# Attention scores and k^T v in four quadrants of the matmul array, with a new map of PSUM banks and a new issue order for the opening

## The chip, the core and the metric

The kernel runs on one core of one Trainium2 chip. The metric is device time in microseconds (us), launch to end. A core has five engines with queues of their own: TensorE (PE, matmuls), VectorE (DVE), ScalarE (ACT), GpSimd (POOL) and SyncE (SP, which issues the DMAs here). Matmuls write to PSUM, which DVE and ACT read.

## What is computed

A linear attention with a decaying state, then two MLPs, all in float32. Four batches, 8 heads, 768 steps, 48 channels a head; the attention's output is laid out as 3072 tokens of 384.

```python
for t in range(S):
    cur = einsum('bhd,bhe->bhde', u * k[t], v[t])
    y[t] = einsum('bhd,bhde->bhe', r[t], state + cur)
    state = w[t][..., None] * state + einsum('bhd,bhe->bhde', k[t], v[t])
x = y as (3072, 384)
h = x @ w_in;  x = (h * sigmoid(1.702 * h)) @ w_out          # d_ff 2048
h = x @ w2_in; solu = h * softmax(h)                         # d_ff 1024
out = (layernorm(solu) * g_ln) @ w2_out
```

## The kernel before, in words

The attention is done in chunks of 64 steps. A *unit* is two chunks of one batch, 128 tokens with all 8 heads; there are 24 units, six (UB) to a batch. Both chunks of a unit lie side by side on the partitions: the first chunk's channels on partitions 64 to 111, the second's on 0 to 47.

The steps of a unit, with the names by which the issue list calls them and the lines of their instructions: loads (Lrkw, Ln, La, Lb); the front, with the running product of the decays (F1, line 134, DVE), r scaled by it (F2 line 140 on POOL, F4 line 146 on DVE), its inverse (F3, lines 153 to 155) and k scaled by that (F5, line 162); the bonus of the diagonal (B on POOL, lines 177 and 178; BR on DVE; BV on POOL, line 201, into `vd`); the transpose of k (ST, `turn_k`, line 213) and its copy to SBUF (SK, `copy_k`, line 218, ACT); the scores k r (SA, `scores`, lines 226 and 227); the masked product that takes them out of PSUM (M0 and M1, `masked`, line 232, DVE); k^T v (D, `states`, lines 253 to 266, or in two parts DA and DB for the first four units); the update of the state (U1, U2, `update`, lines 283 and 286, DVE); the mix with v (X, `mix`, lines 296 and 297); its sum with the bonus (V, `total`, line 303, DVE); the transpose of the result (T, line 311); and its split in a high and a low half (O line 320 on ACT, OL line 326 on DVE). A star in the list, as in OL:2*, moves a DVE step to PE (lines 330 and 331 for OL) and ACT.

A float32 matmul of the program shows as two matmul rows and two weight loads in the profile, so 16 products of the scores are 32 rows.

The attention has three PSUM banks. `three` makes them of a double tile `two` and a single tile `one`: bank 0 is the upper half of `two`, bank 1 is `one`, bank 2 the lower half of `two`, and 3 stands for all of `two`. The dependencies between instructions are found by the framework from the tiles that they touch. From unit 6 on, k's transpose lies in bank 0, the scores in 1, the mix in 2, the result's transpose in 1, and k^T v in 2 and 0.

The first MLP (w_in, w_out) goes over blocks of units, `BLOCKS`: three of two units, then six of three. For each block and each of 16 slices f of d_ff: `rise` (h in the list, line 496, 9 matmuls), `gelu` (e, lines 504 and 506, ACT), `rest` (g, line 511, DVE) and `fall` (o, line 521, 9 matmuls). Its weights arrive as raw 64-bit words that are unpacked in the opening: Lw (load), N0 on ACT, N1 to N3 on DVE (lines 387 to 392), H on ACT, C on DVE (line 423).

Two things set the order. Up to the end of the third block each engine's queue follows `START`, a list written out by hand in the order of issue; it covers units 0 to 8 entirely, most of unit 9, and all unpacking. After that a loop over blocks 3 to 7 and f runs: at each f it issues rise, gelu, rest, then the attention steps that `steps_of` puts there, and then the fall of two slices before. For unit i, `one` (transpose of k, copy, scores of unit i+1; mix of unit i; masked products of i+1; sum of i) stands at f = 1, 6 or 11, and `two` (transpose of the result of i; k^T v of i+1; split of i; update of i+1) three slices later. So the scores of units 10 to 23 are issued in the loop, those of 6 to 9 by the list. The second MLP follows with the whole core to itself, and the change doesn't touch it.

Of the kernel before, what the change touches and what calls it, by code (L numbers as in the profile page):

```python
# [11 lines left out]
ALU = mybir.AluOpType  # L12
# [3 lines left out]
H, D, C = 8, 48, 64  # L16
HD = H * D
# [26 lines left out]
C:4 N0:7 H:5 N2:6 F3:4 h0:4 V:3* La:4 T:3 O:3 o0:1 OL:3* N3:6 o0:3 h1:0 F5:4 F4:4 SA:4 ST:4 N1:7 e0:4 e1:0 g0:4 Lw:8  # L44
h1:1 C:5 g1:0 Lw:9 N2:7 o1:0 h1:2 H:6 N0:8 N1:8 N3:7 SK:4 o0:4 e1:1 H:7 N2:8 g1:1 C:7 Lw:10 La:5 Ln:4 o1:1 N3:8 N0:9
e1:2 N1:9 g1:2 h1:3 e1:3 N2:9 N0:10 D:4 Lb:5 g1:3 h1:4 N3:9 N1:10 e1:4 H:9 o1:3 Lrkw:5 Lrkw:6 C:6 h0:5 e0:5 Lw:12 g1:4
o1:4 h1:5 o1:2 M0:4 e1:5 Lw:11 g0:5 h1:6 U1:4 N2:10 B:4 BR:4 o0:5 BV:4 N3:10 Lw:13 g1:5 h1:7 e1:6 e1:7 H:10 M1:4 X:4
H:8 g1:6 o1:6 F1:6 N0:12 h0:6 e0:6 g1:7 o1:7 h0:7 U2:4 o1:5 C:9 C:10 g0:6 o0:6 C:8 N1:12 N0:11 F1:5 e0:7 g0:7 h1:8
h0:8 La:6 V:4 T:4 F3:5 Ln:5 e1:8 e0:8 g1:8 g0:8 o0:7 O:4 h0:9 N2:12 N0:13 OL:4 e0:9 g0:9 N1:11 N1:13 N2:11 o1:8 N3:12
h1:9 h0:10 e1:9 g1:9 o0:8 o0:9 e0:10 Lw:15 H:12 N3:11 H:11 h1:10 o1:9 e1:10 F4:6 F2:6 F2:5 F4:5 g0:10 F5:5 o0:10 N0:15  # L50
ST:5 C:11 h0:11 g1:10 C:12 N2:13 B:5 h0:12 SK:5 e0:12 e0:11 D:5 F3:6 N3:13 SA:5 g0:11 g0:12 Lw:14 N0:14 o1:10 N1:14
# [17 lines left out]
class Attention:  # L69
# [150 lines left out]
    def scores(self, i):  # L220
        nc, s = self.nc, self.st[i]
# [629 lines left out]
```

## Time and profile before

| | us |
|---|---|
| median of 3 runs | 766.41 |
| lowest and highest | 765.92, 767.46 |
| the profiled execution | 765.8 |
| its span in the profile | 763.7 |
| PE busy, of the span | 745.3 |
| DVE busy | 497.4 |
| ACT busy | 305.0 |
| POOL busy | 154.8 |

The opening (the list) goes from 0 to about 178 us, the loop with the attention and the first MLP to about 495, the last block of the first MLP to about 527, the second MLP to the end. In the profile PE is the matmuls and PEld the weight loads beside them. A row of the order in time gives the start, the length, engine, line, operation, output and inputs, the number of instructions merged, and in brackets the idle time of the engine before it and what ended it.

### The profile page before, as it was taken

How to read it: one execution, taken by the hardware profiler on the slowest of the kernel's cores; microseconds unless marked ns; L12 is line 12 of the kernel's file. 1: busy time of each engine (PE TensorE's matmuls, PEld its weight loads, DVE VectorE, ACT ScalarE, POOL GpSimd, SP SyncE). 2: the span in 40 equal slices, each digit the busy share in tenths (PEclk: the TensorE clock that was granted, in tenths of full speed). 3: DMA queues.
4: the chain of work that ended last, by engine and by line, in shares of the span. 5: the costliest groups of instructions: out<-in, count | busy, mean ns of one | idle time of the engine just before them, and what ended most of it. 6: DMA issues, size and time to landing. Idle time of an engine off the chain costs nothing.

```text
span 763.7 us, 15400 instructions
## 1 busy us (share of the span) xinstructions
PE 745.3 (98%) x6350; PEld 700.5 (92%) x6350; DVE 497.4 (65%) x849; ACT 305.0 (40%) x660; POOL 154.8 (20%) x158
## 2 busy tenths in 40 slices
PE   4899999999999999999999999999999999999998
PEld 3679999999999999999999999999999999999987
DVE  8989998885656665556466562388655555555553
ACT  2455453333222322322322322466544444444443
POOL 5530403622222222222022220031000000000000
PEclk9999999999999999999999999999999999999999
DMA  8656733324221222222222100342000000000000
GB/s 276 195 204 187 219 126 94 95 74 121 74 73 48 62 67 72 73 73 66 55 75 73 38 6 2 112 137 83 1 22 21 22 21 22 22 21 22 21 32 32
DMA packets 26102, 58.03 MB, mean 76 GB/s; under 512 B 3408, under 2 KB 18768, under 8 KB 26032
## 3 DMA queue, kind: packets, MB, share of 16 engines
q1 hardware_dynamic: 26032, 57.04, 25.2%
q8 instruction: 50, 0.82, 0.4%
q14 instruction: 20, 0.16, 0.1%
HBM read 52.31 MB, written 4.72 MB: 75 GB/s over the span
## 4 chain that ended last, share of the span: by engine, by line
PE 95%; DVE 3%; DMA 1%; issue 1%; ACT 0%; SPq 0%; DVEq 0%
PE acc L521 27%; PE h L496 26%; PE o L614 13%; PE left L561 7%; PE right L561 6%; PE att L296 3%; PE att L226 3%; PE right L601 1%; PE left L601 1%; PE att L213 1%; PE att L253 1%; PE att L311 1%; PE att L262 1%; DVE P L134 1%; DMA x2b<-in_w 1%
## 5 line engine op out<-in xcount | busy, mean ns | idle before, releaser
L521 PE MATMUL acc<-gh,w 128*128 128x384 f32 (+1 forms) x864 | 223.2, 322 | 0.0
L496 PE MATMUL h<-xTh,w 128*128 128x384 f32 (+1 forms) x864 | 180.1, 318 | 0.0
L504 ACT ACTIVATE gh<-h 128x384 fp32r<-128x384 f32 (+1 forms) x144 | 65.6, 456 | 271.3 <-PE h L496 263.9
L511 DVE TENSOR_TENSOR gl<-h,gh 128x384 fp32r<-128x384 f32 (+1 forms) x144 | 73.1, 510 | 145.5 <-ACT h L506 145.0
L521 PEld LDWEIGHTS acc<-gh,w 128*128 128x128 f32 x864 | 152.6, 189 | 2.3
L496 PEld LDWEIGHTS h<-xTh,w 128*128 128x128 f32 x864 | 142.8, 189 | 1.1 <-ACT w L421 0.5
L521 PE MATMUL acc<-gl,w 128*128 128x384 f32 (+1 forms) x432 | 137.2, 317 | 0.3 <-DVE gl L511 0.3
L496 PE MATMUL h<-xTl,w 128*128 128x384 f32 (+1 forms) x432 | 90.4, 317 | 0.0
L521 PEld LDWEIGHTS acc<-gl,w 128*128 128x128 f32 x432 | 81.6, 189 | 0.5 <-DVE gl L511 0.5
L496 PEld LDWEIGHTS h<-xTl,w 128*128 128x128 f32 x432 | 72.0, 189 | 0.0
L140 POOL TENSOR_TENSOR R<-rkw,P 64x512 f32<-64x512 f32 x24 | 30.7, 1281 | 202.2 <-DVE P L134 163.4
L614 PE MATMUL o<-w,xTh 128*128 128x384 f32 x384 | 70.5, 334 | 0.0
L614 PEld LDWEIGHTS o<-w,xTh 128*128 128x128 f32 x384 | 67.0, 188 | 0.2
L506 ACT ACTIVATE h<-h 128x384 f32<-128x384 f32 (+1 forms) x144 | 65.0, 451 | 0.0
L201 POOL TENSOR_TENSOR vd<-vs,dg 64x384 f32<-64x384 f32 x48 | 43.4, 904 | 98.4 <-PE att L311 61.4
L591 POOL TENSOR_TENSOR sm<-sm,mhalf 128x1 f32<-128x1 f32 x24 | 13.2, 548 | 218.6 <-DVE sm L590 218.6
L614 PE MATMUL o<-w,xTl 128*128 128x384 f32 x192 | 43.0, 346 | 0.0
L586 ACT ACTIVATE e<-q,sm 128x1024 f32<-128x1024 f32 x24 | 27.7, 1153 | 29.9 <-DVE sm L589 29.4
L561 PE MATMUL right<-w,x2h 128*128 128x512 f32 x144 | 37.1, 392 | 0.0
L561 PE MATMUL left<-w,x2h 128*128 128x512 f32 x144 | 37.0, 392 | 0.0
L226 PE MATMUL att<-R,rkw 48*64 48x64 f32 x368 | 27.1, 225 | 8.8 <-DVE rkw L162 8.8
L226 PEld LDWEIGHTS att<-R,rkw 48*64 48x64 f32 x368 | 23.9, 138 | 11.7 <-DVE rkw L162 8.8
(158 smaller groups left out, 1252.0 us busy)
## 6 DMA issues: line engine op xcount, KB each, us to landing
rkw<-in_rkw SPq DMA_DIRECT2D x22, 676.4 KB, 5.4
x2b<-in_w SPq DMA_DIRECT2D x16, 768.0 KB, 4.9
vs<-in_vn SPq DMA_DIRECT2D x48, 96.0 KB, 4.4
nr<-in_nat SPq DMA_DIRECT2D x24, 192.0 KB, 3.3
nk<-in_nat SPq DMA_DIRECT2D x24, 192.0 KB, 2.4
out<-ob SPq DMA_DIRECT2D x24, 192.0 KB, 1.9
raw<-in_w2o SPq DMA_DIRECT2D x8, 384.0 KB, 3.5
v<-in_v2n SPq DMA_DIRECT2D x24, 96.0 KB, 2.0
```

The costliest lines, as they stand in the source:

```text
L140: (e or self.nc.gpsimd).tensor_tensor(out=heads(R1[0:64]), in0=heads(s["rkw"][0:64, 0:HC]), in1=heads(s["P"])[0:64, :, 0:C], op=ALU.mult)
L201: nc.gpsimd.tensor_tensor(out=heads(vd[q:q + 64]), in0=heads(vt[q:q + 64]), in1=dg[q:q + 64].unsqueeze(2).to_broadcast([64, H, D]), op=ALU ...
L226: nc.tensor.matmul(out=A[0:64, c], lhsT=kt[64:112, c], rhs=R0[64:112, c], start=True, stop=True)
L296: mm(out=y[0:64, e], lhsT=s["R0"][0:112, c], rhs=s["vs0"][0:112, e], start=one, stop=one or h == 7)
L496: nc.tensor.matmul(out=h_ps, lhsT=W1[f][:, ws + c * 128:ws + (c + 1) * 128], rhs=xs[:, c, tok], start=n == 0, stop=n == 8)
L504: nc.scalar.activation(out=gh, in_=h_ps, func=AF.Gelu_apprx_sigmoid)
L506: return nc.scalar.activation(out=h_ps, in_=h_ps, func=AF.Gelu_apprx_sigmoid)
L511: nc.vector.tensor_tensor(out=gl_, in0=g, in1=gh.bitcast(F32), op=ALU.subtract)
L521: nc.tensor.matmul(out=a, lhsT=W1[f][:, ws + e * 128:ws + (e + 1) * 128], rhs=gs, start=first and n == 0, stop=last and n == 2)
L561: nc.tensor.matmul(out=h_ps[:, b * 512:(b + 1) * 512], lhsT=xs[:, c], rhs=W2I[c][wb][:, b * 512:(b + 1) * 512], start=n == 0 and c == 0, s ...
L586: nc.scalar.activation(out=e, in_=q, func=AF.Square, bias=sm[:, 3:4], accum_out=sm[:, 4:5])
L614: nc.tensor.matmul(out=O[i], lhsT=(lo if n == 2 else hi)[:, f * 128:(f + 1) * 128], rhs=W2O[f][n == 1], start=n == 0 and f == 0, stop=n == ...
```

## The change

`QUADS = UB` marks unit 6. From there on, the scores of heads 0 to 3 are written to the first 256 columns of bank 2 and those of heads 4 to 7 to the first 256 of bank 0, and the four products of one turn (two chunks, two groups of heads) use four different quadrants of the array: rows 64 to 111 or 0 to 47, columns 0 to 63 or 64 to 127. The masked product of a chunk is done in two instructions of four heads. The mix goes to columns 256 to 447 of the same two banks, and k's transpose to bank 1. For k^T v without parts (units 4 to 23) the four products of a pair of heads are issued in turn, where before two loops of two followed each other. `START` is ordered anew, with the same entries.

```diff
     def turn_k(self, i):
-        s["kT"] = self.bank(i, 0)
+        s["kT"] = self.bank(i, 0 if i < QUADS else 1)
...
     def scores(self, i):
-        A = s["A"] = self.bank(i, 1)
-        for h in range(H):
-            c = slice(h * C, (h + 1) * C)
-            nc.tensor.matmul(out=A[0:64, c], lhsT=kt[64:112, c], rhs=R0[64:112, c], start=True, stop=True)
-            nc.tensor.matmul(out=A[64:128, c], lhsT=kt[0:48, c], rhs=R1[0:48, c], start=True, stop=True)
...
+        P, Q = self.bank(i, 2)[:, 0:4 * C], self.bank(i, 0)[:, 0:4 * C]
+        s["A"] = [[(P[0:64], 0, 4), (Q[64:128], 4, 4)], [(P[64:128], 0, 4), (Q[0:64], 4, 4)]]
+        for h in range(4):
+            c, d = slice(h * C, (h + 1) * C), slice((h + 4) * C, (h + 5) * C)
+            mm(out=P[0:64, c], lhsT=kt[64:112, c], rhs=R0[64:112, c], start=True, stop=True)
+            mm(out=P[64:128, c], lhsT=kt[0:48, c], rhs=R1[0:48, c], start=True, stop=True)
+            mm(out=Q[0:64, c], lhsT=kt[0:48, d], rhs=R1[0:48, d], start=True, stop=True)
+            mm(out=Q[64:128, c], lhsT=kt[64:112, d], rhs=R0[64:112, d], start=True, stop=True)
...
     def masked(self, i, b):
+        for a, h, n in s["A"][b]:
+            a = a.rearrange("p (h t) -> p h t", h=n)
+            m = self.mask[q:q + 64] if h == 0 else self.mask[64 - q:128 - q]
+            self.nc.vector.tensor_tensor(out=heads(R[q:q + 64])[:, h:h + n], in0=a,
+                                         in1=m.unsqueeze(1).to_broadcast([64, n, C]), op=ALU.mult)
...
     def states(self, i, chunk=None):
+        if first:
+            for p in range(4):
+                mm(out=Dx[64:112, c], lhsT=kTs[0:64, p, 64:112], rhs=vs0[0:64, e], start=True, stop=True)
+                mm(out=Dx[0:48, c], lhsT=kTs[64:128, p, 0:48], rhs=vs1[64:128, o], start=True, stop=True)
+                mm(out=Dy[0:48, c], lhsT=kTs[0:64, p, 0:48], rhs=v2[0:64, p], start=True, stop=True)
+                mm(out=Dy[64:112, c], lhsT=kTs[64:128, p, 64:112], rhs=v2[64:128, p], start=True, stop=True)
+            return
...
     def mix(self, i, e=None):
-        y = s["y"] = self.bank(i, 1 if i < UB else 2)
+            s["y"] = y = self.bank(i, 3).rearrange("p (b c) -> p b c", b=2)[:, :, 4 * C:4 * C + 4 * D]
+            y = [y[:, h // 4, (h % 4) * D:(h % 4 + 1) * D] for h in range(H)]
...
 START = """
-U2:5 Lrkw:0 Lrkw:1 La:0 F1:0 F2:0 F3:0 F4:0 F5:0 F1:1 F4:1 F3:1 Ln:0 Lcst SA:0 M0:0 ST:0 F5:1 F2:1 SA:1 SK:0 Lw:1 N0:1
-Lb:0 N1:1 B:0 BR:0 BV:0 Lw:0 Ln:1 N2:1 N0:0 N1:0 La:1 DA:0 U1:0* ST:1 DB:0 SK:1 N2:0 Lrkw:2 M1:0 B:1 Ln:2 B:2 N3:0
-X:0* Lb:1 U2:0* V:0* T:0 O:0 F1:2 H:0 M0:1 F4:2 Lw:2 DA:1 U1:1* OL:0* N0:2 DB:1 Lrkw:3 BR:1 BR:2 C:0* M1:1 F3:2 Lb:2
-BV:1 X:1* V:1* Lw:3 U2:1* T:1 N1:2 O:1 F5:2 ST:2 N2:2 La:3 La:2 N3:1 Lw:4 SK:2 OL:1* N3:2 Lw:5 F2:2 SA:2 F1:3 H:2 H:1
-F3:3 h0:0 e0:0 g0:0 DA:2 U1:2* N0:3 C:1* h0:1 DB:2 M0:2 BV:2 Ln:3 M1:2 X:2* Lrkw:4 N1:3 N2:3 e0:1 F4:3 F2:3 N0:4 N3:3
-Lw:6 N0:5 Lb:3 g0:1 F5:3 H:3 C:2* h0:2 U2:2* N1:4 ST:3 B:3 V:2* T:2 O:2 N1:5 N2:4 o0:0 C:3 e0:2 h0:3 e0:3 N3:4 N2:5
-SK:3 OL:2* F1:4 F2:4 g0:2 g0:3 SA:3 BR:3 DA:3 o0:2 N0:6 U1:3* DB:3 Lw:7 M1:3 M0:3 N1:6 N3:5 U2:3* BV:3 X:3* Lb:4 H:4
...
+Lrkw:0 F1:0 F3:0 F2:0 F4:0 F5:0 SA:0 Lrkw:1 F1:1 F3:1 Ln:0 Lcst ST:0 B:0 Lw:1 N0:1 M1:0 F5:1 M0:0 La:0 Ln:1 F4:1 F2:1
+N1:1 SK:0 Lb:0 DA:0 Lw:0 BR:0 La:1 U1:0* DB:0 B:1 Ln:2 SA:1 ST:1 BR:1 N2:1 U2:0* N0:0 N1:0 N2:0 N3:0 M1:1 BV:0 SK:1
+X:0* V:0* T:0 Lb:1 DA:1 O:0 H:0 OL:0* C:0* N3:1 Lrkw:2 U1:1* DB:1 F1:2 M0:1 B:2 BR:2 U2:1* Lw:2 N0:2 BV:1 X:1* Lrkw:3
+V:1* F3:2 N1:2 T:1 O:1 OL:1* F5:2 N2:2 F4:2 ST:2 N3:2 Lw:3 F1:3 N0:3 N1:3 La:2 SK:2 h0:0 e0:0 g0:0 Lb:2 Ln:3 N2:3 Lw:4
+DA:2 U1:2* F2:2 F4:3 F2:3 H:2 H:1 SA:2 M0:2 M1:2 C:1* Lw:5 h0:1 F3:3 DB:2 U2:2* Lrkw:4 BV:2 X:2* B:3 e0:1 Lb:3 N0:4
+V:2* g0:1 N3:3 Lw:6 C:2* N1:4 h0:2 T:2 F5:3 N2:4 H:3 C:3 La:3 N0:5 N1:5 o0:0 O:2 h0:3 e0:2 N3:4 Lw:7 ST:3 N2:5 F1:4
+g0:2 BR:3 OL:2* SA:3 M1:3 SK:3 e0:3 DA:3 U1:3* o0:2 M0:3 DB:3 F2:4 g0:3 H:4 C:4 N0:6 La:4 N0:7 U2:3* N1:6 N3:5 N2:6
...
```

`total` and `turn` follow the new places; units 0 to 5 keep theirs.

## Rows read from the trace of the kernel before

**Rows 1.** The page's part 1: busy us, share of the span, instructions.
```profile
PE 745.3 (98%) x6350; PEld 700.5 (92%) x6350; DVE 497.4 (65%) x849; ACT 305.0 (40%) x660; POOL 154.8 (20%) x158
```
**Rows 2.** The page's part 4: shares of the chain that ended last, by line.
```profile
PE acc L521 27%; PE h L496 26%; PE o L614 13%; PE left L561 7%; PE right L561 6%; PE att L296 3%; PE att L226 3%; PE right L601 1%; PE left L601 1%; PE att L213 1%; PE att L253 1%; PE att L311 1%; PE att L262 1%; DVE P L134 1%; DMA x2b<-in_w 1%
```
**Rows 3.** Busy time by stretch: stretch and us, then busy us of each engine.
```profile
0.00:60.00 60.00, 45.42 (x548) 34.51 (x549) 53.28 (x73) 26.08 (x50) 28.59 (x26) 1.00 0.69 218
60.00:178.00 118.00, 117.69 (x1383) 114.82 (x1382) 104.30 (x164) 50.92 (x127) 35.33 (x32) 1.00 0.44 132
178.00:495.00 317.00, 316.90 (x2969) 306.07 (x2969) 176.12 (x279) 95.29 (x230) 68.41 (x68) 1.00 0.23 63
```
**Rows 4.** Waits of PE, 0 to 190 us: waiter, awaited: us, times, longest.
```profile
PE att L226 <- DVE rkw L162: 8.8, 1, 8.8
...
PE att L330 <- ACT kTs L218: 1.2, 1, 1.2
```
**Rows 5.** Order in time, PE: scores of unit 16, of unit 11, and their mixes.
```profile
306.80 0.27 PE L226 MATMUL att<-R,rkw 48*64 48x64 f32 x1
...
306.90 0.22 PE L226 MATMUL att<-R,rkw 48*64 48x64 f32 x1
...
307.73 0.22 PE L227 MATMUL att<-R,rkw 48*64 48x64 f32 x1
307.97 0.26 PE L296 MATMUL att<-vs,R 112*64 112x48 f32 x1
...
202.90 0.22 PE L227 MATMUL att<-R,rkw 48*64 48x64 f32 x1
203.04 0.26 PE L296 MATMUL att<-vs,R 112*64 112x48 f32 x1
```
**Rows 6.** Order in time, PE: k^T v of one unit.
```profile
296.12 0.24 PE L253 MATMUL att<-vs,kTs 64*48 64x48 f32 x1
...
296.20 0.20 PE L253 MATMUL att<-vs,kTs 64*48 64x48 f32 x1
...
296.35 0.24 PE L262 MATMUL att<-v,kTs 64*48 64x48 f32 x1
...
296.43 0.20 PE L253 MATMUL att<-vs,kTs 64*48 64x48 f32 x1
296.43 0.20 PE L262 MATMUL att<-v,kTs 64*48 64x48 f32 x1
296.44 0.20 PE L255 MATMUL att<-vs,kTs 64*48 64x48 f32 x1
296.44 0.20 PE L264 MATMUL att<-v,kTs 64*48 64x48 f32 x1
296.47 0.20 PE L253 MATMUL att<-vs,kTs 64*48 64x48 f32 x1
...
296.71 0.20 PE L264 MATMUL att<-v,kTs 64*48 64x48 f32 x1
```
**Rows 7.** Order in time, ACT: the copies of k's transpose beside Rows 5.
```profile
307.38 0.54 ACT L218 ACTIVATE kTs<-att 128x448 f32<-128x448 f32 x1
...
202.41 0.54 ACT L218 ACTIVATE kTs<-att 128x448 f32<-128x448 f32 x1
```
**Rows 8.** Order in time, DVE: after the scores of unit 16.
```profile
307.99 1.39 DVE L232 TENSOR_TENSOR R<-att,cc 64x512 f32<-64x512 f32 x2
309.42 0.56 DVE L303 TENSOR_TENSOR vd<-att,vd 128x384 f32<-128x384 f32 x1
313.46 0.56 DVE L511 TENSOR_TENSOR gl<-h,gh 128x384 fp32r<-128x384 f32 x1 [3.48 <-ACT h L506]
```
**Rows 9.** Groups by line and shape, DVE: count, busy us, mean ns.
```profile
L511 DVE TENSOR_TENSOR gl<-h,gh 128x256 fp32r<-128x256 f32 x48 | 19.7, 417 | 7.7 <-ACT h L506 7.2
...
L390 DVE SCALAR_TENSOR_TENSOR x2a<-x2b,x2a 128x768 uint32<-128x768 uint32 x16 | 15.9, 994 | 0.1
```
**Rows 10.** Order in time, POOL: a bonus product in the opening.
```profile
11.60 1.93 POOL L177 TENSOR_TENSOR nr<-nr,nk 128x384 f32<-128x384 f32 x1
```

More of the change, by code (lines that the diff above doesn't have):

```diff
@@ L23 @@
 VDB = 1
+QUADS = UB
 DFF2 = NF2 * 128
@@ L47 @@
[L47 to L51, printed above, removed]
@@ L220, in scores, with masked @@
     def scores(self, i):
-        nc, s = self.nc, self.st[i]
+        mm, s = self.nc.tensor.matmul, self.st[i]
         kt, R0, R1 = s["kt"], s["R0"], s["R1"]
-        A = s["A"] = self.bank(i, 1)
-        for h in range(H):
-            c = slice(h * C, (h + 1) * C)
-            nc.tensor.matmul(out=A[0:64, c], lhsT=kt[64:112, c], rhs=R0[64:112, c], start=True, stop=True)
-            nc.tensor.matmul(out=A[64:128, c], lhsT=kt[0:48, c], rhs=R1[0:48, c], start=True, stop=True)
-    def masked(self, i, b, e=None):
+        if i < QUADS:
+            A = self.bank(i, 1)
+            s["A"] = [[(A[0:64], 0, H)], [(A[64:128], 0, H)]]
+            for h in range(H):
+                c = slice(h * C, (h + 1) * C)
+                mm(out=A[0:64, c], lhsT=kt[64:112, c], rhs=R0[64:112, c], start=True, stop=True)
+                mm(out=A[64:128, c], lhsT=kt[0:48, c], rhs=R1[0:48, c], start=True, stop=True)
+            return
[7 more added lines that the diff above has]
+            mm(out=Q[64:128, c], lhsT=kt[64:112, d], rhs=R0[64:112, d], start=True, stop=True)
+    def masked(self, i, b):
         s, q = self.st[i], 64 * b
         R = s["R1" if b else "R0"]
-        (e or self.nc.vector).tensor_tensor(out=heads(R[q:q + 64]), in0=heads(s["A"][q:q + 64]),
-                                            in1=self.mask[q:q + 64].unsqueeze(1).to_broadcast([64, H, C]), op=ALU.mult)
+        for a, h, n in s["A"][b]:
[3 more added lines that the diff above has]
+                                         in1=m.unsqueeze(1).to_broadcast([64, n, C]), op=ALU.mult)
     def states(self, i, chunk=None):
@@ L261, in states @@
             o, c = slice((2 * p + 1) * D, (2 * p + 2) * D), slice(p * D, (p + 1) * D)
-            mm(out=Dy[0:48, c], lhsT=kTs[0:64, p, 0:48], rhs=v2[0:64, p], start=first, stop=first or p == 3)
-            if chunk is None:
-                mm(out=Dy[64:112, c], lhsT=kTs[64:128, p, 64:112], rhs=v2[64:128, p], start=True, stop=True)
-            else:
-                mm(out=Dx[0:48, c], lhsT=kTs[64:128, p, 0:48], rhs=vs1[64:128, o], start=False, stop=p == 3)
+            mm(out=Dy[0:48, c], lhsT=kTs[0:64, p, 0:48], rhs=v2[0:64, p], start=False, stop=p == 3)
+            mm(out=Dx[0:48, c], lhsT=kTs[64:128, p, 0:48], rhs=vs1[64:128, o], start=False, stop=p == 3)
     def update(self, i, b, e=None):
@@ L289, in mix @@
         mm, s = self.nc.tensor.matmul, self.st[i]
-        y = s["y"] = self.bank(i, 1 if i < UB else 2)
         one = e is None
+        if i < QUADS:
+            s["y"] = y = self.bank(i, 1)[:, 0:HD]
+            y = [y[:, h * D:(h + 1) * D] for h in range(H)]
+        else:
+            s["y"] = y = self.bank(i, 3).rearrange("p (b c) -> p b c", b=2)[:, :, 4 * C:4 * C + 4 * D]
+            y = [y[:, h // 4, (h % 4) * D:(h % 4 + 1) * D] for h in range(H)]
         if e is not None:
-            mm(out=y[:, 0:HD], lhsT=self.ident, rhs=s["vd"], start=True, stop=False)
+            mm(out=s["y"], lhsT=self.ident, rhs=s["vd"], start=True, stop=False)
         for h in range(H):
             c, e = slice(h * C, (h + 1) * C), slice(h * D, (h + 1) * D)
-            mm(out=y[0:64, e], lhsT=s["R0"][0:112, c], rhs=s["vs0"][0:112, e], start=one, stop=one or h == 7)
-            mm(out=y[64:128, e], lhsT=s["R1"][:, c], rhs=s["vs1"][:, e], start=one, stop=one or h == 7)
+            mm(out=y[h][0:64], lhsT=s["R0"][0:112, c], rhs=s["vs0"][0:112, e], start=one, stop=one or h == 7)
+            mm(out=y[h][64:128], lhsT=s["R1"][:, c], rhs=s["vs1"][:, e], start=one, stop=one or h == 7)
     def total(self, i, e=None):
-        s = self.st[i]
-        y, vd = s["y"][:, 0:HD], s["vd"]
+        y, vd = self.st[i]["y"], self.st[i]["vd"]
+        if i >= QUADS:
+            vd = vd.rearrange("p (b c) -> p b c", b=2)
         if e is None:
@@ L308, in turn @@
         s = self.st[i]
-        s["xT"] = self.bank(i, 2 if i < UB else 1)
+        s["xT"] = self.bank(i, 2 if i < QUADS else 1)
         for c in range(3):
```

38 lines of the change are left out of this document (21 added, 17 removed).

## Prediction, made before the changed kernel was run

> **What bounds the kernel now.** I read the page's busy table first, then the chain of work that ended last, then busy time by stretch, and only then the order in time of single steps. The page shows TensorE (PE) busy 745.3 of 763.7 us and VectorE (DVE) 497.4 [rows 1]; in the chain, lines 521 and 496 (the first MLP) hold 53% and the attention's products hold the shares that this change touches: line 226 (scores) 3%, line 253 and 262 (k^T v) 2% [rows 2]. Busy time by stretch says where a saved PE microsecond counts: from 178 to 495 us PE is busy 316.90 of 317.00 us while DVE has 176.12, so there the PE alone sets the pace; from 60 to 178 us it is busy 117.69 of 118.00; in the first 60 us only 45.42 [rows 3]. The waits of PE put 8.8 of those 14.6 idle us before the first product, which needs the loads and scans of unit 0, and 1.2 us in one wait on line 330 [rows 4]. So the kernel is PE-bound from about 60 us on, and behind that an opening that waits.
>
> "Busy" hides one thing: a small matmul's row is 0.20 to 0.27 us long, but the next begins much sooner. Costs below are therefore taken from start to start.
>
> **Scores, units 6 to 23.** Before, 16 logical products (32 matmul rows, two for each) alternate between lines 226 and 227, that is between two quadrants of the array. They start from 306.80 to 307.73, 0.93 us: a first interval of 0.10, then (307.73 - 306.90) / 14 = 0.059 us for each pair [rows 5]. Each quadrant thus takes a new matmul every 59 ns. In the change each of four quadrants gets 8 rows in place of 16. If a quadrant keeps its 59 ns with three neighbours active, first to last start is 0.10 + 6 x 0.059, and about 0.02 for the stagger, 0.47 us. Gain 0.46 us a unit, times 18 units 8.3 us.
>
> Whether four quadrants run at once is seen in the kernel before, in k^T v. Its first loop (lines 253, 255) and its second (262, 264) use different quadrants, and the second starts at 296.35 while the first still has rows to go. Between 296.43 and 296.47 all four lines are active, and line 253 still starts every 0.04 us (296.43, 296.47) as it did alone [rows 6]. Four starts fall into 10 ns there. So neighbours cost nothing that this view shows, and products into the same columns of the array and different banks (253 with 264, 255 with 262) go together, as the new scores need.
>
> **k^T v, units 4 to 23.** Because the loops overlap only near the end, the 32 rows start from 296.12 to 296.71, 0.59 us [rows 6]. Taken in turn from the start, each quadrant has 8 rows: 0.08 + 6 x 0.045 + 0.02 = 0.37 us. Gain 0.22 us, times 20 units 4.4 us. In the opening one of these units already overlaps with its neighbour's scores, so I take 4.3.
>
> **Where the banks go.** Before, k's transpose goes to one half of the double tile, and the mix to the other half. The first matmul of the mix starts at 307.97, 0.24 us after the last score, against 0.15 us at 202.90 to 203.04 [rows 5]; the copy of k's transpose (line 218, ScalarE) starts at 307.38 and takes 0.54 us, so it ends at 307.92, 0.05 us before the mix; the one at 202.41 ends at 202.95 [rows 7]. So the mix waits for that copy in five of the 14 units of the loop (0.24 there, 0.15 in the other nine), and would wait in all of them if the scores alone became shorter: this wait is next in line. The change moves the transpose to the single tile, which the mix no longer touches. I take the wait as gone: 5 x 0.09 = 0.45 us, and 0.15 us stays between scores and mix. If it stays, the scores gain almost nothing (a rival below).
>
> **The new wait, on DVE.** Scores and mix now lie in the same two banks, and the masked products of unit i+1 (DVE) stand behind the mix of unit i. They used to start at 307.99, as the mix began [rows 8]; now they start when it ends. The mix would begin at 307.97 - 0.55 = 307.42 (0.46 and 0.09, above) and takes, at the same 0.059 us a pair and 0.22 us for the last row, 1.15 us, so they start near 308.6. They also become four of 64x256 in place of two of 64x512 (1.39 us for the two [rows 8]). The nearest row to a 64x256 from PSUM is line 511 with 128x256, 417 ns [rows 9]: 4 x 0.42 = 1.67 us, 0.28 more a unit; bounds are 1.39 (nothing more) and 2.8 (each as long as now). Behind them queue the sum of line 303 and then the next low half of the GELU (line 511). DVE was idle 3.48 us before that one, at 313.46 [rows 8]. The shift is 0.6 + 0.3 = 0.9 us and that GELU comes 0.55 earlier, together 1.5 us, so it is covered; at 2.8 us it is 2.6, and 0.9 is left. Cost 0 on the path; without that idle time it would be 0.9 us a unit. The scores now write where the previous unit's k^T v lay, which its two updates read; those end two steps of the loop earlier, and the transpose waited for the same reads before. No transfer moves in the loop.
> The page "PSUM — Partial Sum Buffer" of the Trainium skill, section "PSUM bank collisions raise a hardware error", asks for a guard by bank and quadrant, not by address. By that rule the masked products may not start during the mix, although their columns are disjoint; that costs the 1.1 us of the mix on DVE and nothing on PE.
>
> **The opening, nine units set anew.** The new list has the same 564 entries, and the same 45 changes between attention and MLP on PE. I compared queue by queue what stands ahead of the same step. By row durations DVE has about 28.3 us of work before the first rise (h0:0) against 29.2, and 32.3 against 30.2 before the second; by the fourth both have 39.4. PE loses the scores of unit 2 before the first rise, but gets them before the second. One stall goes by construction: OL:2, behind SK:3 in the old list, waited 1.2 us for it (line 330 on 218 [rows 4]); in the new list it stands ahead. On POOL the bonus of unit 1 now stands ahead of unit 0's bonus times v, which seeds the first mix; a bonus is two products, the first of which took 1.93 us in the opening [rows 10], so up to 3.9 us. SP gets unit 0's v behind a weight block, Lw:1, but its first reader comes only after a transpose and a copy. So bounds: at best the 14.6 - 8.8 = 5.8 us of idle time are won back, at worst the 3.9 us of that bonus come onto the path. I take -1.0: the stall removed, less some 0.2 of slips, since the other shifts nearly cancel.
>
> **Sum.** -8.3 - 4.3 - 0.45 - 1.0 = -14.0 us on the profiled execution's 765.8, so 751.8. Its time lies 0.6 below the median of the three runs, 766.41, so the median should go to 752.4 us. A change of 0.2% (1.5 us) is about what a measurement of this kernel can tell from none.
>
> **Rivals.**
> *Matmuls are paced, not quadrants.* If PE can't start them faster than k^T v shows on average, 0.59 / 31 = 19 ns, scores need 31 x 0.019 = 0.59 us: gain 0.34 x 18 = 6.1, k^T v none, the rest as above, -7.6: 758.8. The four starts in 10 ns speak against it; that the burst lasts only three or four rounds speaks for it. 9%.
> The page "TensorE: Matmul & The Clock Gate" of the Trainium skill, section "Wait — 56ns, not 53.3ns?", states such a floor: start to start never below about 25 ns. By that the scores would need 0.78 us and the whole change would give 762.3 (an estimate from that page); the trace disagrees already with 19 ns on average.
> *The mix still waits for the copy of k's transpose.* Then the scores' gain turns into that wait: only 4.3 + 1.0, 761.1. The old bank map speaks for such a link, the new one against it, since the tiles differ. 6%.
> *The opening pays.* POOL's bonus puts 3.9 us on the path in place of -1.0: 757.3. 7%.
> *Slower than before.* The place is the opening, the mechanism DVE: it is busy 53.28 of 60 us there [rows 3], so each weight block whose unpacking on DVE (three steps, 0.99 us for one [rows 9]) is put ahead of an awaited step costs about 3.0 us. Eating the 13 us of the other terms takes more than four such slips; five (15 us) end at 768.4. The counts ahead of the same rises differ by 2.1 at most, against that. 4%.
> The forecast itself has 74%, with its own range 749 to 756: 18 units at 0.42 to 0.50, and an opening between -4 and +2.
>
> **How the numbers follow.** The forecast's range and the paced case and the paying opening lie between 748.5 and 759.0; outside are the mix that still waits (6%), the slower case (4%) and the tails of the forecast, some 8% together. Faster by over 0.2% 0.94, since all cases but the last lie below 764.9; within 0.2% 0.02; slower 0.04.
>
> **What would show it.** Lines of the new scores: 32 rows within 0.47 us; 0.93 or 0.59 says wrong or paced. Rows of k^T v: 0.37 us, all four lines from the start. The first row of the mix 0.15 us after the last score in every unit, and no wait on line 218. The masked products starting after the mix, at about 0.42 us each, and still no PE wait after 60 us. The first 384-wide rise, at 177.9 us before, some 4 us earlier (1.8 scores, 1.2 k^T v, 1.0 opening). The forecast is wrong if quadrants slow each other (intervals over 59 ns) or if the PE stands idle in the opening for longer than 14.6 us.

## The result, and the profile after

The changed kernel takes 753.26 us (median of 5 runs, 752.37 to 754.38) against 766.09 (765.76 to 767.46) for the kernel before in the same session. The ratio is 0.983, with an interval of 0.9816 to 0.9844: about 13 us faster. The forecast was 752.4. The profiled execution of after took 753.76 us with a span of 750.8, so the span went down by 12.8 (763.68 to 750.84).

In the code after, the lines are: scores 238 to 241, masked products 250, k^T v 263 to 266 (in parts 271 to 276), mix 322 and 323, transpose of k 215 and its copy 220, sum 330, transpose of the result 338, OL 357, rise 523, GELU 531, 533 and 538, fall 548.

The busy table of after and its chain by line (shares of the span) answer [rows 1, 2]:

```profile
PE 732.8 (98%) x6350; PEld 688.8 (92%) x6350; DVE 502.2 (67%) x885; ACT 304.0 (40%) x660; POOL 153.3 (20%) x158
...
PE acc L548 28%; PE h L523 27%; PE o L641 13%; PE left L588 7%; PE right L588 7%; PE att L322 3%; PE right L628 1%; PE left L628 1%; PE att L215 1%; PE att L238 1%; PE att L338 1%; PE att L263 1%; PE d L446 1%; PE att L231 0%; PE att L275 0%
```

PE is busy 12.5 us less (745.3 to 732.8), nearly the whole change of the span, with the same 6350 matmul rows: no work left, it lies closer together. The scores' share of the chain fell from 3% (line 226) to 1% (line 238). DVE has 36 instructions more, two for each of 18 units.

Busy time by stretch, after (stretch, us, then busy us and rows of PE, PEld, DVE, ACT, POOL), answers [rows 3]:

```profile
0.00:60.00 60.00, 45.52 (x548) 34.80 (x549) 52.69 (x73) 24.87 (x48) 26.30 (x26) 1.00 0.79 231
60.00:178.00 118.00, 117.83 (x1403) 115.06 (x1402) 107.29 (x177) 52.75 (x132) 37.04 (x32) 1.00 0.43 132
178.00:495.00 317.00, 317.00 (x3023) 306.52 (x3021) 188.96 (x323) 101.72 (x245) 70.74 (x70) 1.00 0.24 66
```

The first 60 us are the same to 0.1 us on PE. From 60 us on PE is as full as before, but gets through more rows in the same time: 3023 in the third stretch where it had 2969. So the gain is denser work behind the opening and no idle time won back. The granted clock is 1.00 in all three stretches (the higher of the two levels), as before.

Where the time went, from the first row of the rise in each block (us from the start of the span), profiled executions:

| | before | after |
|---|---|---|
| first block | 35.71 | 35.84 |
| second block | 63.76 | 63.77 |
| fourth block, the first with 384 columns | 177.94 | 174.88 |
| last block of the first MLP | 486.25 | 473.44 |
| end | 763.68 | 750.84 |

Nothing is gained up to 63.8 us, 3.1 us from there to the fourth block, 9.75 us in the loop (308.31 to 298.56 us), and nothing behind it (277.43 and 277.40 us).

The order in time on PE, scores of unit 11 and the start of the mix (start, length, engine, line), answers [rows 5]:

```profile
198.15 0.27 PE L238 MATMUL att<-R,rkw 48*64 48x64 f32 x1
198.15 0.27 PE L239 MATMUL att<-R,rkw 48*64 48x64 f32 x1
198.16 0.27 PE L240 MATMUL att<-R,rkw 48*64 48x64 f32 x1
198.17 0.27 PE L241 MATMUL att<-R,rkw 48*64 48x64 f32 x1
198.25 0.22 PE L238 MATMUL att<-R,rkw 48*64 48x64 f32 x1
...
198.31 0.22 PE L238 MATMUL att<-R,rkw 48*64 48x64 f32 x1
...
198.62 0.22 PE L241 MATMUL att<-R,rkw 48*64 48x64 f32 x1
198.77 0.26 PE L322 MATMUL att<-vs,R 112*64 112x48 f32 x1
```

All four quadrants start within 0.02 us, each keeps its 0.06 us from one row to the next (198.25, 198.31), and the 32 rows start within 198.62 - 198.15 = 0.47 us. The mix follows 0.15 us after the last score, here and in all 14 units of the loop. The k^T v of one unit, same view, answers [rows 6]:

```profile
209.74 0.24 PE L263 MATMUL att<-vs,kTs 64*48 64x48 f32 x1
209.75 0.24 PE L264 MATMUL att<-vs,kTs 64*48 64x48 f32 x1
209.75 0.24 PE L265 MATMUL att<-v,kTs 64*48 64x48 f32 x1
209.76 0.24 PE L266 MATMUL att<-v,kTs 64*48 64x48 f32 x1
209.82 0.21 PE L263 MATMUL att<-vs,kTs 64*48 64x48 f32 x1
...
210.11 0.20 PE L266 MATMUL att<-v,kTs 64*48 64x48 f32 x1
```

All four lines run from the start, and the 32 rows start within 0.37 us, where before they took 0.59.

The waits of PE in after, 0 to 190 us (waiter, awaited: us in total, times, longest), answer [rows 4]:

```profile
PE att L231 <- DVE rkw L164: 8.5, 1, 8.5
PE att L271 <- DVE vs L125: 3.0, 1, 3.0
PE att L275 <- DVE vs L306: 0.7, 1, 0.7
...
...
PE att L271 <- ACT kTs L220: 0.3, 1, 0.3
```

The 1.2 us of OL:2 behind the copy of k's transpose are gone. In their place stands one of 3.0 us: line 271 is DA:0, and line 125 is a memset on DVE inside `load_v`, the step La:0 of the list, which stands behind M0:0 in the new order and at the head of the old one. None of these waits lies behind 60 us. The list is PE's own; waits of its weight loads stand in that of PEld, to which the reorderings below come back.

DVE in the order of time, from the masked products of unit 11 to the next low half of a GELU (in brackets the idle time ahead and what ended it), answers [rows 8]; the last row is the group of all masked products of that shape (count, busy us, mean ns), which answers [rows 9]:

```profile
199.98 1.73 DVE L250 TENSOR_TENSOR R<-att,cc 64x256 f32<-64x256 f32 x4 [0.72 <-PE att L323]
201.72 0.56 DVE L330 TENSOR_TENSOR vd<-att,vd 128x384 f32<-128x384 f32 x1
...
204.24 0.56 DVE L538 TENSOR_TENSOR gl<-h,gh 128x384 fp32r<-128x384 f32 x1 [1.46 <-ACT h L533]
...
L250 DVE TENSOR_TENSOR R<-att,cc 64x256 f32<-64x256 f32 x72 | 30.3, 421 | 10.7 <-PE att L323 9.5 <-PE att L241 0.5
```

The masked products now wait for the mix (line 323), and the GELU behind them still waits for ScalarE with 1.46 us of DVE to spare.

### The profile page after: what moved, and what is told of

The parts are those of the page before. It is cut to its first block, busy times and chain, and to the rows that moved or that the text cites. A ratio compares the mean times of both kernels' runs of the same rounds, so it can differ in the third digit from the quotient of the medians.

```text
span 750.8 us, 15429 instructions
## 1 busy us (share of the span) xinstructions
PE 732.8 (98%) x6350; PEld 688.8 (92%) x6350; DVE 502.2 (67%) x885; ACT 304.0 (40%) x660; POOL 153.3 (20%) x158
## 4 chain that ended last, share of the span: by engine, by line
PE 96%; DVE 2%; ACT 1%; issue 0%; DMA 0%; ACTq 0%; DVEq 0%
PE acc L548 28%; PE h L523 27%; PE o L641 13%; PE left L588 7%; PE right L588 7%; PE att L322 3%; PE right L628 1%; PE left L628 1%; PE att L215 1%; PE att L238 1%; PE att L338 1%; PE att L263 1%; PE d L446 1%; PE att L231 0%; PE att L275 0%
## 5 line engine op out<-in xcount | busy, mean ns | idle before, releaser
L250 DVE TENSOR_TENSOR R<-att,cc 64x256 f32<-64x256 f32 (+1 forms) x82 | 37.2, 454 | 10.9 <-PE att L323 9.5
L179 POOL TENSOR_TENSOR nr<-nr,nk 128x384 f32<-128x384 f32 x24 | 26.0, 1083 | 43.5 <-DMA nk<-in_nat 42.4
```

What stands on the lines that cost most here:

```text
L179: g.tensor_tensor(out=s["nr"], in0=s["nr"], in1=s["nk"], op=ALU.mult)
L250: self.nc.vector.tensor_tensor(out=heads(R[q:q + 64])[:, h:h + n], in0=a, in1=m.unsqueeze(1).to_broadcast([64, n, C]), op=ALU.mult)
```

## The experiments

All experiments change the kernel after, except the one on the kernel before. A stage is always taken from the profiled execution. The kernel before had a median of 766.98 in the session of the runs on k^T v and the scores and of the first run with both undone, 766.73 in that of the masked products, the opening and the first reordering, and 766.63 in that of the bank of k's transpose, the second run with both undone and both reorderings.

### Each product alone

**k^T v back in two loops.** For each pair of heads the two quadrants of the first chunk pair, then, in a second loop, the other two. Banks and list stay.

```diff
             for p in range(4):
...
                 mm(out=Dx[64:112, c], lhsT=kTs[0:64, p, 64:112], rhs=vs0[0:64, e], start=True, stop=True)
                 mm(out=Dx[0:48, c], lhsT=kTs[64:128, p, 0:48], rhs=vs1[64:128, o], start=True, stop=True)
+            for p in range(4):
...
                 mm(out=Dy[0:48, c], lhsT=kTs[0:64, p, 0:48], rhs=v2[0:64, p], start=True, stop=True)
                 mm(out=Dy[64:112, c], lhsT=kTs[64:128, p, 64:112], rhs=v2[64:128, p], start=True, stop=True)
```

> The changed kernel with k^T v of units 4 to 23 issued in two loops of two quadrants again; all else as changed. My theory, that the gain is the time in which PE starts these products: first to last start goes from 0.37 back to 0.59 us, 20 x 0.22 = 4.4 us longer, 757.7 us. Rival, that the gain comes from the new bank map and issue order: within 1 us of 753.3.

Measured: 757.37 us (0.9881 of before, 0.986 to 0.9903), span 755.1, first to last start 0.58 us in each unit. The step up to the next row took 0.72 us in place of 0.50, so 20 units should cost 20 x 0.215 = 4.3 us; the span grew by 755.06 - 750.84 = 4.2. The interleaving is worth its 4.3 us, and all of it reaches the end.

**Scores in the same banks, from two quadrants.**

```diff
...
-            mm(out=Q[0:64, c], lhsT=kt[0:48, d], rhs=R1[0:48, d], start=True, stop=True)
-            mm(out=Q[64:128, c], lhsT=kt[64:112, d], rhs=R0[64:112, d], start=True, stop=True)
+            mm(out=Q[0:64, c], lhsT=kt[64:112, d], rhs=R0[64:112, d], start=True, stop=True)
+            mm(out=Q[64:128, c], lhsT=kt[0:48, d], rhs=R1[0:48, d], start=True, stop=True)
...
```

The masks and the list of score tiles follow the new places.

> The changed kernel with the scores of units 6 to 23 written to the same two banks, but from two quadrants only, as before. My theory: first to last start goes from 0.48 to 0.93 us, 18 x 0.45 = 8.1 us longer, 761.4 us, and the mix still begins 0.15 us after the last score, since it no longer waits for the copy of k's transpose. Rival, that the copy of k's transpose was the limit and moving it gave the gain: 753 to 755 us.

Measured: 762.37 us (0.9938, 0.9919 to 0.9957), span 759.1, that is 8.3 more than after; 18 units x (1.078 - 0.625) us from the first score to the mix are 8.2. The scores' rows again take 0.93 us, and the mix still starts 0.15 us after the last. So the gain is the quadrants, not the banks.

**Both undone**, in two sessions, to see what the bank map and the list are worth without the quadrants:

> The changed kernel with both reverted, scores from two quadrants and k^T v in two loops; left are the bank map, the masked products in four, and the new issue order. My theory: what is left is worth 0.45 us in the loop (the wait of the mix) and nothing in the opening, so 765.6 us against 766.1 before, and the two reverts add up, 4.4 + 8.1. Rival, that map and order carry several us: 761 to 764.

> Scores from two quadrants and k^T v in two loops once more, with more rounds: it bounds what bank map and issue order are worth together. First seen as 0.9982 of the time before, 0.9972 to 0.9992. By my theory 0.45 us and nothing from the opening, 0.9994; by my prediction 0.45 + 1.0, 0.9981.

Measured: 765.11 us in 10 runs (0.9982, 0.9972 to 0.9992) and 765.82 in 12 (0.9983, 0.9972 to 0.9994); spans 763.1 and 762.7. What is left of the change is 0.0017 x 766.6 = 1.3 us, give or take 0.8. In the loop it is 308.31 - 307.74 = 0.57 and 308.31 - 307.79 = 0.52 us, which the next experiment names. The rest isn't all the opening's. By the medians of the span the two kernels differ by 1.3 us in the first session (764.6 to 763.3) and by 0.45 in the second (764.5 to 764.05), so outside the loop the span gains 0.8 us or nothing. Another 0.35 us lies outside the span: time less span is 2.13 and 2.15 us before, and 1.79 with both undone, in the medians of the two sessions. No run here names its cause.

**The transpose of k in a bank of its own, in the kernel before.** Scores and transpose swap banks for the units of the loop; nothing else.

```diff
-        s["kT"] = self.bank(i, 0)
+        s["kT"] = self.bank(i, 0 if i < 10 else 1)
...
-        A = s["A"] = self.bank(i, 1)
+        A = s["A"] = self.bank(i, 1 if i < 10 else 0)
```

> The kernel before, in which only the loop's 14 units have k's transpose in the single tile and their scores in its old place, the upper half of the double tile; two quadrants as before. My theory: the mix waits for the copy of k's transpose because both lie in the double tile. So here the mix begins 0.15 us after the last score in all 14 units (before: 0.24 in five), and the masked products, now in the mix's tile, start after it. 0.45 us less, 765.6 us. Rival, that the 0.24 us are PE's own: still 0.24 in five units.

Measured, one run: 766.73 us beside 766.63. At the end it does not show, since the opening of this run was later (second block's rise at 64.69 where the kernel before has 63.76). In the loop it does: 307.79 us against 308.31, 0.52 less. The time from first score to mix went from 1.110 to 1.078 us in the mean, 14 x 0.032 = 0.45 us. On PE, last score, first and last matmul of the mix, and then DVE (order in time, this kernel, where line 297 is the mix and 232 the masked product):

```profile
185.34 0.22 PE L227 MATMUL att<-R,rkw 48*64 48x64 f32 x1
185.49 0.26 PE L296 MATMUL att<-vs,R 112*64 112x48 f32 x1
...
186.41 0.22 PE L297 MATMUL att<-vs,R 128*64 128x48 f32 x1
...
186.70 1.39 DVE L232 TENSOR_TENSOR R<-att,cc 64x512 f32<-64x512 f32 x2 [1.05 <-PE att L297]
```

The mix stands 0.15 us behind the scores in every unit, so the 0.45 us of the forecast are right. And the masked products, which before started as the mix began [rows 8], now wait for its end, although scores and mix lie here in different banks, the two halves of one double tile.

### What decides about four quadrants

**k^T v quadrant by quadrant.** The same 16 products, but all four pairs of one quadrant before the next.

```diff
             for p in range(4):
...
                 mm(out=Dx[64:112, c], lhsT=kTs[0:64, p, 64:112], rhs=vs0[0:64, e], start=True, stop=True)
+            for p in range(4):
...
                 mm(out=Dx[0:48, c], lhsT=kTs[64:128, p, 0:48], rhs=vs1[64:128, o], start=True, stop=True)
+            for p in range(4):
...
                 mm(out=Dy[0:48, c], lhsT=kTs[0:64, p, 0:48], rhs=v2[0:64, p], start=True, stop=True)
+            for p in range(4):
...
                 mm(out=Dy[64:112, c], lhsT=kTs[64:128, p, 64:112], rhs=v2[64:128, p], start=True, stop=True)
```

> The changed kernel with k^T v of units 4 to 23 issued quadrant by quadrant, all four products of one before the next. In the kernel before, the second loop began when about ten instructions ahead of it had not yet started, so my theory is that PE looks only some 10 to 14 instructions ahead: about two quadrants at a time, first to last start 0.55 to 0.75 us, 4 to 8 us longer than the changed kernel, 757 to 761. Rival, that PE looks ahead over all 64 instructions of the step, so that the order among them is free: 0.37 us and 753.3.

Measured: 765.68 us in 10 runs (0.9984, 0.9974 to 0.9995). I had expected 757 to 761, and it is far worse: 1.01 us from first to last start in each unit, where two loops have 0.58 and turns 0.37. This edit alone eats nearly all of the change. The order in time of this kernel, PE and its weight loads (PEld), lines 263 and 266 the first two quadrants and 269 the third:

```profile
195.82 0.34 PEld L263 LDWEIGHTS att<-vs,kTs 64*48 64x48 f32 x6 [0.17 <-issue]
195.82 0.42 PE L263 MATMUL att<-vs,kTs 64*48 64x48 f32 x5
196.04 0.16 PEld L266 LDWEIGHTS att<-vs,kTs 64*48 64x48 f32 x2
196.04 0.24 PE L266 MATMUL att<-vs,kTs 64*48 64x48 f32 x1
...
196.08 0.20 PE L263 MATMUL att<-vs,kTs 64*48 64x48 f32 x1
196.08 0.12 PEld L263 LDWEIGHTS att<-vs,kTs 64*48 64x48 f32 x1
...
196.13 0.12 PEld L263 LDWEIGHTS att<-vs,kTs 64*48 64x48 f32 x1
...
196.26 0.16 PEld L269 LDWEIGHTS att<-v,kTs 64*48 64x48 f32 x2
```

The second quadrant starts at 196.04, when two weight loads (196.08, 196.13) and three matmuls of the first have yet to start: five instructions of its sixteen. The third starts 0.22 us later, at 196.26, at the same point of the second. With two loops, the second loop starts (211.54 us in that trace) when five instructions are left in each of the two quadrants of the first, ten in all, and so it does in the kernel before; a count over the whole queue would not fit both runs, a count for each quadrant does. The free quadrants thus stand idle while the first has more than about five instructions to go, whatever they could do. My reading is that an instruction whose quadrant already has about five waiting stops everything behind it; in turns, no quadrant ever has that many ahead of the others. What holds them I can't see, only when the next one starts.

### DVE and the opening

**Masked products by head**, 16 instructions a unit in place of 4, to take the cover of the new wait away.

```diff
...
-            self.nc.vector.tensor_tensor(out=heads(R[q:q + 64])[:, h:h + n], in0=a,
-                                         in1=m.unsqueeze(1).to_broadcast([64, n, C]), op=ALU.mult)
+            step = n if n == H else 1
+            for g in range(0, n, step):
+                self.nc.vector.tensor_tensor(out=heads(R[q:q + 64])[:, h + g:h + g + step], in0=a[:, g:g + step],
+                                             in1=m.unsqueeze(1).to_broadcast([64, step, C]), op=ALU.mult)
```

> The changed kernel with the masked products of units 6 to 23 taken one head at a time, 16 instructions a unit in place of four. From 687 ns for 64x512 and 421 for 64x256 a 64x64 is worth some 0.22 us, so 3.5 us a unit in place of 1.7. My theory: DVE behind the mix is covered, the low half of the GELU comes at most 0.4 us late in the loop and PE needs it only two rises on, so within 1 us of 753.3. Rival, that the DVE queue is next in line: each microsecond that exceeds the idle time shows, 14 x 0.4 = 5.6 us, 758.9.

Measured: 754.41 us (0.984, 0.9824 to 0.9857). The group of that line in this kernel:

```profile
L252 DVE TENSOR_TENSOR R<-att,cc 64x64 f32<-64x64 f32 x288 | 45.4, 217 | 10.5 <-PE att L325 9.5 <-PE att L241 0.2
```

16 x 0.217 = 3.5 us a unit, twice the 1.7 of after. The loop stayed at 298.63 us (298.56 in after): 14 units x 1.8 us more on DVE cost nothing there. The fourth block's rise came at 175.99, 1.1 us later (1.25 counted from the second block's rise), so in the units of the list the cover is thinner. DVE's new work is hidden, with at least as much again to spare in the loop.

**Unit 0's v at the head of the list**, to remove the 3.0 us wait that I had not foreseen.

```diff
-Lrkw:0 F1:0 F3:0 F2:0 F4:0 F5:0 SA:0 Lrkw:1 F1:1 F3:1 Ln:0 Lcst ST:0 B:0 Lw:1 N0:1 M1:0 F5:1 M0:0 La:0 Ln:1 F4:1 F2:1
+Lrkw:0 La:0 F1:0 F3:0 F2:0 F4:0 F5:0 SA:0 Lrkw:1 F1:1 F3:1 Ln:0 Lcst ST:0 B:0 Lw:1 N0:1 M1:0 F5:1 M0:0 Ln:1 F4:1 F2:1
```

> The changed kernel with the load of unit 0's v, which also clears a piece of it on DVE, moved to the head of the list. The new order let PE wait 3.0 us for that clearing. My theory: the opening is set by the DVE queue, where the first update stands behind the same work as before, so the 3.0 us move elsewhere: 0 to 0.5 us gained, 752.8 to 753.3. Rival, that the wait is on the path: 750.3.

Measured: 753.06 us (0.9818, 0.9803 to 0.9833), the same as after. The waits of PE, 0 to 190 us, in this kernel:

```profile
PE att L271 <- ACT kTs L220: 2.5, 2, 2.2
PE att L275 <- DVE vs L306: 2.2, 1, 2.2
```

The wait for the memset has gone and its time stands at the next two steps of the same unit (2.2 behind the copy, 2.2 behind the update in place of 0.7). A wait of 3.0 us in the list of waits was worth nothing.

**The old list up to the fifth unit**, the new one behind it (its first 231 entries, through h0:5).

```diff
-Lrkw:0 F1:0 F3:0 F2:0 F4:0 F5:0 SA:0 Lrkw:1 F1:1 F3:1 Ln:0 Lcst ST:0 B:0 Lw:1 N0:1 M1:0 F5:1 M0:0 La:0 Ln:1 F4:1 F2:1
...
+U2:5 Lrkw:0 Lrkw:1 La:0 F1:0 F2:0 F3:0 F4:0 F5:0 F1:1 F4:1 F3:1 Ln:0 Lcst SA:0 M0:0 ST:0 F5:1 F2:1 SA:1 SK:0 Lw:1 N0:1 Lb:0
...
```

> The changed kernel with the first 231 entries of the old list (through h0:5), then the rest in the new order. My theory: the first rise of the second block starts at 63.8 us with either list, so the new order of this part is worth nothing: within 0.7 us of 753.3. Rival, what I predicted: the old part has the wait of 1.2 us again and is 1.0 us slower, 754.3.

Measured: 755.73 us (0.9852, 0.9837 to 0.9867), span 752.6, 1.8 more than after. Up to the second block both lists are equal: that rise starts at 63.60 us with the old part and at 63.77 in after. The 1.8 us come later, at the seam, where a fall waits for the low half of a GELU (waits of PE, this kernel):

```profile
PE acc L547 <- DVE gl L537: 1.9, 1, 1.9
...
PE att L356 <- ACT kTs L219: 1.2, 1, 1.2
```

So this run prices the seam of two lists, and of the opening itself it says only that the old first part is as good as the new. The wait of OL:2 for SK:3 is back in it (1.2 us) and the second block starts no later for it.

### Changing the order of half and full height

Height is how many rows of the array a product uses, width how many columns. In after, PE goes from the transpose of k (112 x 128, the full array) to the scores (48 x 64, a quadrant), to the mix (112 or 128 x 64, full height and half width) and to the fall (128 x 128). The first of two reorderings puts the transpose and its copy behind the mix, next to the fall, which uses the full array as well.

```diff
-                    at.turn_k(i + 1)
-                    at.copy_k(i + 1)
...
+                    at.turn_k(i + 1)
+                    at.copy_k(i + 1)
```

> The changed kernel with the transpose of k and its copy put behind the mix in the loop's step of 14 units. In the loop transpose, scores and mix cost 2.29 us (5 units) or 2.41 (9), with what the rise before and the fall behind them lose; in the opening, where the order is scores, mix, transpose, the same costs about 2.2. My theory: going from a full-height transpose to half-height scores costs PE 0.1 to 0.2 us that the order scores first spares, 14 times, 1 to 2 us in all: 751.3 to 752.3. Rival, that the order within the step is free or that k's copy comes late for k^T v: 753.3 or more.

Measured: 752.83 us (0.981, 0.9796 to 0.9825). The loop went from 298.56 to 297.04 us. Per unit, from the first row of a step to that of the next: transpose 0.51 to 0.37, the rise ahead of the group 1.62 to 1.66, the fall behind it 1.64 to 1.63; together 0.12, times 14 units 1.6 us against the 1.5 measured.

Most of that is not the change of height. Here are, for after, the waits of the weight loads (PEld) from 175 to 495 us, then the order in time of two units, one at f = 6 and one at f = 1; the last two lines are the waits with the scores first:

```profile
PEld att L215 <- DVE rkw L164: 2.1, 9, 0.2
...
196.87 0.69 DVE L164 TENSOR_TENSOR rkw<-rkw 112x512 f32<-112x512 f32 x1
197.61 0.39 PEld L215 LDWEIGHTS att<-cc,rkw 112*128 112x128 f32 x4 [0.23 <-DVE rkw L164]
197.61 0.60 PE L215 MATMUL att<-cc,rkw 112*128 112x112 f32 x4
...
235.03 0.69 DVE L164 TENSOR_TENSOR rkw<-rkw 112x512 f32<-112x512 f32 x1
238.64 0.52 PEld L215 LDWEIGHTS att<-cc,rkw 112*128 112x128 f32 x4
...
PEld att L238 <- DVE rkw L164: 2.2, 9, 0.2
PEld att L238 <- issue: 1.2, 5, 0.3
```

In nine of the 14 units (f = 6 and 11) the transpose's first weight load waits for F5 (k scaled, line 164, DVE), which ends 0.05 us before it. In the five units at f = 1, F5 ended 3 us earlier, and the load starts 0.18 us ahead of its matmul. PE shows no idle time, because the row of the rise's last matmul still runs; but rise and transpose together take 2.17 us in the nine units and 2.04 in the five, and 9 x 0.13 = 1.2 us. With the scores first, the same nine wait for F5, but all 14 units start 0.27 us after the rise's last row, so the wait is covered. Slice by slice, the nine units gained 0.16 us each (1.40 in all) and the five 0.02 each. The 1 to 2 us that I expected came, then, mostly for another reason: a wait on DVE that I had overlooked. An earlier F5 in the old order was not tried.

The second does the same three slices later, with k^T v ahead of the result's transpose:

```diff
-                at.turn(i)
...
+                at.turn(i)
```

> The order scores, mix, transpose of k in the loop, and k^T v ahead of the transpose of the result as well. The first of these shortened the loop by 1.5 us. In the loop the transpose of the result takes 0.42 us ahead of k^T v, in the opening 0.30 behind it, and the fall that follows loses 0.07 in place of 0.13, while the rise loses 0.09: some 0.08 us a unit, 14 times 1.1 us. My theory: 2.6 us below the changed kernel, 750.7. Rival, that the order of these is free: equal to the run of scores first.

Measured, with both reorderings: 751.68 us in 5 runs (0.9797, 0.9782 to 0.9812), span 748.1. The loop is 296.45 us, 0.6 less again, where I had expected 1.1. The order in time on PE of this kernel, last of k^T v, transpose, fall:

```profile
208.87 0.20 PE L266 MATMUL att<-v,kTs 64*48 64x48 f32 x1
209.01 0.55 PE L338 MATMUL att<-cc,vd 128*128 128x128 f32 x3
209.31 0.42 PE L548 MATMUL acc<-gh,w 128*128 128x384 f32 x1
```

The transpose takes 0.30 us to the next step, where it took 0.42 ahead of k^T v in after, but the rise ahead of k^T v grew from 1.57 to 1.66 and the fall shrank from 1.69 to 1.67: 0.05 a unit is left, 0.6 us for 14. Transpose and rise came as I had counted them; from the fall I had expected 0.06 us and it gave 0.02. This version beats both kernels; the changed kernel itself, in the same session:

> The changed kernel itself, on the same chip as the three others: 0.983 of the time before, 753.3 us by all theories.

Measured: 753.48 us in 4 runs (0.9823, 0.9811 to 0.9836), so 751.68 lies 1.8 us below it, with intervals that just touch (0.9812 and 0.9811); the loops of the two profiles differ by 2.2 us.

## Why the prediction was right

**The whole.** 752.4 forecast, 753.26 measured: 0.9 us apart, inside the forecast's own range. By steps:

| step | forecast, us | measured, us |
|---|---|---|
| scores, 18 units | -8.3 | -8.2 (18 x 0.453); -8.3 by the run with two quadrants |
| k^T v, 20 units | -4.3 | -4.3 (20 x 0.215); -4.2 by the run with two loops |
| mix no longer waits | -0.45 | -0.45 (14 x 0.032); loop -0.52 in the kernel before |
| DVE | 0 | 0 |
| opening, new order | -1.0 | 0.0 at the second block, in the profiles |

The first three sum to 12.95, and the span fell by 12.84.

**The quadrants.** The step that carried it was to read costs from start to start, and from a stretch of 40 ns in which all four lines of k^T v were active [rows 6] that neighbours cost nothing. Both held: 0.47 and 0.37 us were forecast and are in the rows. The rival of paced matmuls, with 0.59 us for the scores, falls with the same rows: 31 intervals in 0.47 us are 15 ns each, below its 19. The Trainium skill, page "TensorE: Matmul & The Clock Gate", section "Wait — 56ns, not 53.3ns?", states about 25 ns as the least from start to start; the trace disagrees where the products go to four quadrants, with 15 ns here and 0.37 / 31 = 12 ns in k^T v. Within one quadrant rows start no closer than 59 and 45 ns.

**The mix.** It starts 0.15 us behind the scores in all 14 units, and no wait on the copy of k's transpose is left there: the rival in which it still waits, 761.1, is out.

**DVE.** Forecast were four instructions of 417 ns that start behind the mix and are covered; measured 421 ns and a start at 199.98, behind the mix's last row. The cover was real: twice the time costs nothing in the loop. The reason I gave beside it needs care. The page "PSUM — Partial Sum Buffer" of the Trainium skill, section "PSUM bank collisions raise a hardware error", asks for a guard by bank and quadrant, and the order in after agrees; but in the kernel before with swapped banks the same wait appears between different banks of one tile. So the wait follows the tile, and none of these runs shows whether the bank alone would ask for it.

**The opening is the term that was mis-sized.** I counted -1.0: the 1.2 us stall of OL:2 less 0.2 of slips. The stall went, and the second block's rise stayed at 63.77 us (63.76 before). From there to the fourth block 3.06 us were gained, and the quadrants explain them alone: four units of scores x 0.45 and six of k^T v x 0.215 are 3.1. The opening up to the second block, split at the first rise (stretch, us, then busy us and rows of PE, PEld, DVE, ACT, POOL; the first two lines are before, the others after):

```profile
0.00:35.71 35.71, 22.34 (x282) 16.44 (x282) 32.19 (x42) 11.60 (x22) 19.35 (x18) 1.00 0.76 235
35.71:63.76 28.05, 26.84 (x302) 21.82 (x299) 24.81 (x37) 15.85 (x33) 9.23 (x8) 1.00 0.61 199
...
0.00:35.84 35.84, 21.62 (x250) 15.82 (x251) 29.98 (x41) 10.31 (x20) 16.54 (x18) 1.00 0.86 239
35.84:63.77 27.93, 27.67 (x332) 22.75 (x331) 26.44 (x39) 16.84 (x34) 9.77 (x8) 1.00 0.71 223
```

The failed step is "the other shifts nearly cancel". The prediction saw that the scores of unit 2 move from ahead of the first rise to behind it, and set the one against the other. But ahead of the first rise PE has 13 us to spare, so 32 rows fewer there brought no gain that shows, while behind it the same rows filled the time that the stall had left (282 to 250 rows, and 302 to 332, where a row that straddles the edge counts on both sides). That stretch became 0.1 us shorter, not 1.2: it lasts 27.91 to 27.95 us in all ten profiles with the new list, and 28.03 to 28.04 in the three with the old first part, where the stall stands.

Other rows of PE's waits in the opening move as well: with v loaded first, the 3.0 us reappeared at the next steps. I also overlooked that La:0, which I followed on SP alone, carries a memset on DVE, and that it was moved behind M0:0 there; the wait of 3.0 us that this made is such a row. The size of the term isn't settled to better than about a microsecond: in the profiles of kernels with this same list the first rise starts anywhere from 35.3 to 37.4 us, and by the medians of the two runs with both products undone, 1.3 +/- 0.8 us less the 0.5 of the mix, the new order may be worth something between nothing and 1.6 us, some 0.35 of it outside the span. What sets the time up to the first rise, with DVE busy 32.19 of its 35.71 us before and 29.98 of 35.84 in after, and PE waiting 8.5 us ahead of the first product, was not tried.

**The rivals in the opening.** No 3.9 us for the bonus on POOL and no five slips on DVE show: PE has 45.52 us busy in the first 60, 45.42 before. The new list was also needed by the new bank map, since in the old order a transpose of k (ST:6) stands ahead of the sum (V:5) that still reads bank 1, to which it would go; that is argued from the lists, not run.

## What to carry over

Cost small matmuls from start to start, by quadrant, and look for a moment in the old trace where the wanted neighbours already run together: a few rows were enough to price this change to 1 us. Issue products for different quadrants in turn, one each, since the same sixteen products cost 0.37 us in turn, 0.58 in two loops and 1.01 quadrant by quadrant. A wait in an opening that is full of waits has no price until a run takes it away, and work moved out of a stretch with idle time need not gain anything there. A step of a loop in which PE is 100% busy counts in full, once for each unit; but busy doesn't mean that nothing waits, so read the weight loads' waits too.

## What the hardware showed that was not expected

- **The reach of the issue order is short.** With the eight rows of one quadrant issued in a row, the next quadrant starts only when about five instructions of the first are left (196.04 us beside 196.08 and 196.13); 14 units of it made the loop 307.34 us in place of 298.56.
- **Matmuls of different quadrants start out of order and very close.** In the kernel before, line 262 starts at 296.35 while earlier-issued rows of line 253 start at 296.43 [rows 6]; in after 32 rows start in 0.47 and 0.37 us.
- **A change of the array's shape costs about 0.09 us, whichever way it goes.** Rows of one shape follow each other after 0.06 us in the scores and the mix, 0.045 in k^T v and 0.17 in the rise. The mix starts 0.15 us after the last row of the scores (same width, other height), the fall 0.15 after the mix (same height, other width; 199.69 to 199.84 in after) and 0.135 after k^T v. Scores and k^T v in the reordered kernels, and the mix of the last unit in after, start 0.27 us after a rise, a fall 0.17 after it, with no loss. The page "TensorEngine Tiling (Array Packing)" of the Trainium skill, section "Key Properties", says that a change of tiling mode drains the engine; the trace agrees, and this is its price here.
- **The two reorderings didn't save a change.** They won 2.1 us over 14 units, but three changes around the scores stay three, and two around k^T v stay two. About 1.2 us are the nine waits on DVE that are now covered.
